# FFN begun on four row tiles, spectral middle lagged by one pair, pass two opened with gate halves: one change in three parts to a fused gradient kernel

## Chip, cores, metric

One core of one Trainium2 chip. The metric is the device time of one execution in microseconds (us), the median of several.

## The reference, cut to what matters

```python
x = A_x                                              # 2048 x 576, bf16
g = sigmoid((x * gate_w).sum(-1, keepdims=True))
a = irfft2(rfft2(x) * (w_r + 1j * w_i))              # spectral branch
b = (gelu(x @ w_gate) * (x @ w_up)) @ w_down         # FFN, 576 -> 4608 -> 576
out = g * a + (1 - g) * b
# the kernel returns out and the gradients of x, w_r, w_i, w_gate, w_up, w_down, gate_w
```

## The kernel before

Pass one walks 18 groups of 256 FFN columns; a group has 8 steps of two row tiles, 144 steps in all. A row tile is 128 rows. A step is 30 matmuls (`H_mm`), a chain of ScalarE and VectorE work (`H_ew1`, `H_ew2`) and three stores. Weight gradients of the last group (`pend`) and the spectral branch are threaded between the steps: `want` says how many of 203 spectral "slots" (small pieces of work; a "gap" is an empty one) must have been emitted by each half step, and `side` is a queue of VectorE items, of which some are emitted after each step. Pass two computes the down projection (b) and the gradient of x from stored activations, read back by DMA transposes (`pin`). Every engine runs its instructions in the order of emission.

The start, in which everything of x and of the output gradient is loaded and transposed first:

```python
for t0 in range(0, T, 4):
    nc.scalar.dma_start(xn[:, t0:t0 + 4, :], x_v[:, t0:t0 + 4, :])      # ScalarE issues x
...
wts = {0: load_w(0)}
for t in range(T):
    load_dOT(t)                       # two DMA transposes each, on the sync queue (LD)
...
for t0 in range(0, T, 4):
    LD.dma_start(dB[:, t0:t0 + 4, :], do_v[:, t0:t0 + 4, :])
...
build_D(nc, tb, unit, res)            # VectorE arguments, then ScalarE sines
x_chunk(0); build_R(nc, tb, unit, 0)
x_chunk(4); build_R(nc, tb, unit, 3)
x_chunk(8); build_R(nc, tb, unit, 6)
x_chunk(12)                           # then the gate of all 16 row tiles
```

The spectral middle. `s2` makes X and G of a pair of rows; after its last one the 12 product items of the pair go into `side`; `s1` transforms a product, and if it has not been emitted yet, it empties `side` up to it ("forced"):

```python
        side.extend(products(p))      # halve G, m1, m2, comb m, halve m + ready, n1, n2, comb n + ready, o1, o2, comb o, out
...
def s1(p, key, ii, dst):
    def f():
        while (p, key + "_ready") not in st:
            side.pop(0)()
        ...                           # four matmuls on st[p, key], ScalarE copy, store
for p in range(T // 2):
    out += [s2(p, "x", 0), s2(p, "x", 1), s2(p, "g", 0), s2(p, "g", 1)]
    out += [s1(p - 1, "n1", 0, scr_p2), s1(p - 1, "n1", 1, scr_p2)]      # three gaps for p = 0
    out += [s1(p, "m1", 0, scr_p1), s1(p, "m1", 1, scr_p1)]
...
for _ in range(3):                    # after each FFN step
    if side: side.pop(0)()
```

Pass two: seven pieces of the down projection (72 matmuls each) run first. Of the six loads of the transposed w_up (`wuT`) one goes ahead of the first piece and one behind each of the first five.

## Time and profile before

| | before |
|---|---|
| median time, us | 1625.99 (1625.65 to 1626.97, 4 runs) |
| span of the profiled run, us (a fifth run; its time was 1629.32) | 1627.5 |
| PE busy | 1523.0 us, 94% |
| granted TensorE clock, mean | 0.98 |
| start of FFN step 0 / 8 / 143 (square activation) | 38.0 / 124.6 / 1139.6 |
| end of the weight gradients | 1169.05 |

PE is nearly always busy, so the idle stretches, and the stretches at half clock that follow them, are what can be gained or lost. The square activation is the first ScalarE instruction of a step; its start times mark the steps and cut the kernel into stages that can be compared between versions. "Half clock" is taken from the clock record in the trace, which knows two values here, 1.0 and 0.5.

### The profile page before, as it was taken

What the parts mean: (1) busy time and instruction counts of PE and PEld (TensorE: products, weight loads), DVE (VectorE), ACT (ScalarE), POOL (GpSimd) and SP (SyncE); (2) the same over time, 40 slices, a digit from 0 to 9 for tenths busy, and PEclk for the clock granted to TensorE, in tenths of its full rate; (3) what the DMA queues carried; (4) which work ended last, traced back from release to release, by engine and by line L of the source; (5) the groups of instructions that cost most, each with busy time, mean ns of one, the idle gap of its engine ahead of it and who ended that gap; (6) DMA issues with size and microseconds to landing.
All of it is one profiled execution on the core that took longest, in us unless ns stands there. A gap on an engine that the chain in (4) does not pass through costs nothing.

```text
span 1627.5 us, 32888 instructions
## 1 busy us (share of the span) xinstructions
PE 1523.0 (94%) x13310; PEld 1276.6 (78%) x13310; DVE 893.2 (55%) x2287; ACT 628.1 (39%) x1096; POOL 26.3 (2%) x58
## 2 busy tenths in 40 slices
PE   4479999999899899899999999999898999999998
PEld 3357888888788788788888888888775777777776
DVE  3566767668789789777666667678123111111010
ACT  5355555545555555545545555545100000000000
POOL 1000000000000000000000000000000000000000
PEclk9789999999999999999999999999998999999999
DMA  6524234244434434334335345264799988887773
GB/s 131 136 65 112 80 103 111 80 121 130 128 116 143 124 118 140 103 109 123 109 94 135 103 116 130 87 156 127 212 208 211 171 172 159 165 165 162 149 150 70
DMA packets 512569, 212.66 MB, mean 131 GB/s; under 512 B 317984, under 2 KB 506272, under 8 KB 512416
## 3 DMA queue, kind: packets, MB, share of 16 engines
q1 hardware_dynamic: 510208, 203.48, 52.4%
q0 software_dynamic: 1632, 4.72, 0.8%
q10 hardware_dynamic: 576, 2.36, 0.6%
q8 instruction: 104, 1.70, 0.5%
q14 instruction: 49, 0.40, 0.1%
HBM read 40.89 MB, written 93.82 MB: 83 GB/s over the span
## 4 chain that ended last, share of the span: by engine, by line
PE 62%; issue 24%; DVE 5%; SPq 4%; ACT 3%; DMA 1%; POOL 1%; POOLq 0%; DVEq 0%; ACTq 0%
PE hps L286 25%; PE wps L365 15%; PE wps L349 7%; PE pf L610 3%; PE pf L405 3%; PE acc L780 2%; PE wps L376 2%; SPq L206 1%; SPq L207 1%; PE pf L596 1%; PE pf L594 1%; DMA pin<-scr 1%; SPq L720 1%; POOL out_dram L833 0%; ACT q L297 0%
## 5 line engine op out<-in xcount | busy, mean ns | idle before, releaser
L286 PEld LDWEIGHTS <-xT 128*128 128x128 bf16 x2880 | 286.3, 99 | 40.3
L822 PEld LDWEIGHTS <-pin 128*128 128x128 bf16 x2304 | 226.0, 98 | 61.6 <-DMA pin<-scr 3.8
L365 PEld LDWEIGHTS <-xn 128*128 128x128 bf16 x2304 | 223.9, 98 | 30.3 <-issue 3.6
L286 PE MATMUL hps<-wg_g,xT 128*128 128x256 bf16 x1440 | 187.0, 279 | 0.0
L286 PE MATMUL hps<-wu_g,xT 128*128 128x256 bf16 x1440 | 183.6, 275 | 0.0
L286 PE MATMUL hps<-wdT_g,dOT 128*128 128x256 bf16 x1440 | 181.1, 273 | 0.0
L299 DVE TENSOR_SCALAR s<-q 128x512 bf16<-128x512 bf16 x144 | 42.1, 292 | 229.0 <-ACT q L297 228.9
L780 PE MATMUL acc<-wd_all,pin 128*128 128x288 bf16 x1152 | 148.5, 293 | 13.1 <-DMA pin<-scr 13.1
L286 PEld LDWEIGHTS <-dOT 128*128 128x128 bf16 x1440 | 141.1, 98 | 16.6
L822 PE MATMUL acc<-wgT,pin 128*128 128x288 bf16 x1152 | 150.7, 288 | 3.5 <-DMA pin<-scr 3.5
L349 PE MATMUL wps<-dB,A 128*128 128x288 bf16 x1152 | 152.5, 287 | 0.0
L780 PEld LDWEIGHTS <-pin 128*128 128x128 bf16 x1152 | 114.5, 100 | 45.6 <-DMA pin<-scr 14.6
L822 PE MATMUL acc<-wuT,pin 128*128 128x288 bf16 x1152 | 149.1, 287 | 0.0
L830 DVE SCALAR_TENSOR_TENSOR f32t<-gwf,dlog,f32t 128x576 f32<-128x576 f32 x16 | 13.1, 818 | 238.3 <-ACT f32t L828 238.3
L349 PEld LDWEIGHTS <-A 128*128 128x128 bf16 x1152 | 112.7, 98 | 27.6
L365 PE MATMUL wps<-dHu,xn 128*128 128x256 bf16 x1152 | 131.7, 273 | 0.0
L365 PE MATMUL wps<-dHg,xn 128*128 128x256 bf16 x1152 | 131.5, 273 | 0.0
L297 ACT ACTIVATE q<-hps 128x512 bf16<-128x512 f32 x144 | 85.9, 597 | 111.3 <-PE hps L286 111.3
L828 ACT COPY f32t<-acc 128x576 f32<-128x576 f32 x16 | 10.2, 638 | 279.1 <-PE acc L822 279.1
L304 ACT ACTIVATE om<-s 128x512 bf16<-128x512 bf16 x144 | 91.0, 632 | 57.8 <-DVE s L300 57.8
L307 DVE TENSOR_TENSOR da<-hps,omg 128x512 bf16<-128x512 f32 x144 | 99.3, 690 | 2.8 <-PE hps L286 2.7
L305 ACT ACTIVATE s<-s 128x512 bf16<-128x512 bf16 x144 | 90.7, 630 | 4.6
(163 smaller groups left out, 1755.7 us busy)
## 6 DMA issues: line engine op xcount, KB each, us to landing
scr<-A SPq DMA_DIRECT2D x144, 128.0 KB, 1.8
scr<-dHg SPq DMA_DIRECT2D x144, 128.0 KB, 1.9
scr<-dHu SPq DMA_DIRECT2D x144, 128.0 KB, 1.9
out_dram<-dw SPq DMA_DIRECT2D x72, 128.0 KB, 1.9
out_dram<-dwd SPq DMA_DIRECT2D x36, 144.0 KB, 2.4
wd_all<-in_B_w_down_dram SPq DMA_DIRECT2D x3, 1728.0 KB, 13.5
scr_p<-Vt SPq DMA_DIRECT2D x32, 144.5 KB, 2.4
Vp<-scr_p SPq DMA_DIRECT2D x16, 289.0 KB, 3.0
```

The costliest lines, as they stand in the source:

```text
L286: nc.tensor.matmul(pt[:, tt, :], lhsT=xt[:, ci, tp * TPB + tt, :], rhs=w[:, ci, :], start=(ci == 0), stop=(ci == 4))
L297: nc.scalar.activation(q[:], hg[:], ACT.Square)
L299: V.tensor_scalar(s[:], q[:], A_GELU, 1.0, op0=ALU.mult, op1=ALU.add)
L304: nc.scalar.activation(om[:], s[:], ACT.Sigmoid, scale=-2.0 * C_GELU)
L305: nc.scalar.activation(s[:], s[:], ACT.Sigmoid, scale=2.0 * C_GELU)
L307: V.tensor_tensor(da[:], da_ps[:], omg32[:, t0:t0 + TPB].unsqueeze(2).to_broadcast([P, TPB, FG]), op=ALU.mult)
L349: nc.tensor.matmul(wps[:, :288], lhsT=tl(0, t)[:, fch * P:(fch + 1) * P], rhs=dB[:, t, h * 288:(h + 1) * 288], start=(t == 0), stop=(t == ...
L365: nc.tensor.matmul(wps[:, cc, :], lhsT=xn[:, t, (c0 + cc) * P:(c0 + cc + 1) * P], rhs=tl(k, t), start=(t == 0), stop=(t == T - 1))
L405: nc.tensor.matmul(yps[:, c, :DF], lhsT=src[:, ci, t, :], rhs=tb.Dt[ci][:, c, :], start=(ci == 0), stop=(ci == 4))
L610: nc.tensor.matmul(yps[:, h, :288], lhsT=Z[:, lc, c, :], rhs=tb.At[lc][:, c, h * 288:(h + 1) * 288], start=(n == 0), stop=(n == 5))
L780: nc.tensor.matmul(bps[:, h, :288], lhsT=At[:, r, :], rhs=wd_all[:, fc, h * 288:(h + 1) * 288], start=(fc == 0), stop=(fc == NFC - 1))
L822: nc.tensor.matmul(xps[:, h, :288], lhsT=src[:, r, :], rhs=wT[:, h * 288:(h + 1) * 288], start=(n < 2), stop=(n >= 4 * NFC - 2))
```

## The change

Its intent: begin the FFN when four row tiles of x are there and bring in the rest between the first steps; give each product of the spectral middle a pair's distance to its use; cover the loads of pass two with matmuls whose weights are already on the chip. The core of the diff, with cuts as `...` and long lines condensed:

```diff
-    build_D(nc, tb, unit, res)
-    x_chunk(0)
-    build_R(nc, tb, unit, 0)
-    ... (x_chunk 4, 8, 12, build_R 3, 6, gate of all tiles)
+    x_chunk(0, (0, 1, 2))
+    build_D(nc, tb, unit, res)
+    build_R(nc, tb, unit, 0)
+    run_late(tb)                        # sines are now emitted late, after the arguments
+    gate(0)
...
+    def early_x(k):                     # after steps 0, 1, 2: x chunk, gate, dOT; k == 3: dB loads
+    def early_tables():                 # after step 3
+        for t0 in range(3, T, 3):
+            build_R(nc, tb, unit, t0)
+        build_B(nc, tb, unit, res)
+        run_late(tb)
+        wts[1] = load_w(1)
...
     def want(step, half):
-        n = max(0.0, min(EARLY, 1.5 * (2 * step + half - 1)))     # EARLY = 24
-        h = 2 * (step - NT) + half
-        if h > 0:
-            n += (n_slots - EARLY) * h / (2.0 * (LAST - NT))
+        h = 2 * step + half
+        if h <= 2 * NT:
+            n = max(0, h - 3)
+        else:
+            n = 2 * NT - 3 + (n_slots - 2 * NT + 3) * (h - 2 * NT) / (2.0 * (LAST - NT))
...
-            out += [s1(p - 1, "n1", ...)] * 2 ; [s1(p, "m1", ...)] * 2
+            if p > 0:
+                out += [s1(p - 1, "m1", 0, scr_p1), s1(p - 1, "m1", 1, scr_p1)]
+                out += [s1(p - 1, "n1", 0, scr_p2), s1(p - 1, "n1", 1, scr_p2)]
...
-            for _ in range(3):
+            for _ in range(2):
                 if side:
...
-        LEAD = 7                        # pass two: b0 to b6, a wuT load ahead of b0 and behind b0 to b4
+    jobs = [("g", 0), ("g", 1), ("b", 0), ("b", 1), ("b", 2), ("u", 0), ("u", 1)]
+    ensure()                            # six pins, ahead of wd_all
+        for k in range(NB):
+            for r0 in (0, 6):
+                load_wuT(k, r0)         # all six, ahead of the first job
```

Beside these: the tile At of the inverse transform is stored in memory between its uses and one shared buffer fewer is kept (19), the absolute value in `build_D` moves from ScalarE to VectorE, dB is scaled in steps 6 to 9, x is loaded by the sync queue and not by ScalarE, a first small sine is run at once, some copies of the x chunks change engine, and the weight gradients of the first group run in another order.

More of the change, by code (lines that the diff above doesn't have):

```diff
@@ L35 @@
 FCH = FG // P
-NUNIT = 20
+NUNIT = 19
 IMM = bass.MemoryType
@@ L81, in iotas, with run_late @@
     nc.vector.memset(tb.npi[:], -math.pi * EPS_SCALE)
-    return tb
+    tb.warm = res.tile([P, 1], F32, name="warm")
+    nc.scalar.activation(tb.warm[:], tb.halfpi[:], ACT.Sin)
+    tb.late = []
+    return tb
+def run_late(tb):
+    while tb.late:
+        tb.late.pop(0)()
 def build_D(nc, tb, unit, res):
@@ L102, in build_D, with sines @@
         o = unit([n, 2, DF], name="Dt")
-        nc.scalar.activation(y[:], X[:], ACT.Abs)
-        nc.scalar.activation(o[:, :, 0, :], y[:], ACT.Sin, bias=tb.halfpi[:], scale=-step)
-        nc.scalar.activation(o[:, :, 1, :], X[:], ACT.Sin, scale=-step * EPS_SCALE)
+        V.scalar_tensor_tensor(y[:], X[:], -1.0, X[:], op0=ALU.mult, op1=ALU.max)
+        def sines(o=o, X=X, y=y):
+            nc.scalar.activation(o[:, :, 0, :], y[:], ACT.Sin, bias=tb.halfpi[:], scale=-step)
+            nc.scalar.activation(o[:, :, 1, :], X[:], ACT.Sin, scale=-step * EPS_SCALE)
+        tb.late.append(sines)
         tb.Dt += [o[:, c] for c in range(n)]
@@ L121, in build_R, with sines @@
     o = unit([n, 3, P], name="Rt")
-    nc.scalar.activation(o[:, :, 0, :], C[:], ACT.Sin, bias=tb.pi[:], scale=-step)
-    nc.scalar.activation(o[:, :, 1, :], X[:], ACT.Sin, bias=tb.npi[:], scale=step)
-    nc.scalar.activation(o[:, :, 2, :], X[:], ACT.Sin, bias=tb.pi[:], scale=-step)
+    def sines():
+        nc.scalar.activation(o[:, :, 0, :], C[:], ACT.Sin, bias=tb.pi[:], scale=-step)
+        nc.scalar.activation(o[:, :, 1, :], X[:], ACT.Sin, bias=tb.npi[:], scale=step)
+        nc.scalar.activation(o[:, :, 2, :], X[:], ACT.Sin, bias=tb.pi[:], scale=-step)
+    tb.late.append(sines)
     tb.Rt += [o[:, t] for t in range(n)]
@@ L146, in build_B, with sines @@
     step = 2.0 * math.pi / 16 * EPS_SCALE
-    nc.scalar.activation(o[:, 0, :], XC[:, 0, :], ACT.Sin, bias=tb.npi[:], scale=step)
-    nc.scalar.activation(o[:, 1, :], XC[:, 1, :], ACT.Sin, bias=tb.pi[:], scale=-step)
-    nc.scalar.activation(o[:, 2, :], XC[:, 0, :], ACT.Sin, bias=tb.pi[:], scale=-step)
     tb.B = res.tile([P, 3, P], BF16, name="Btab")
-    V.tensor_tensor(tb.B[:], o[:], mask[:].unsqueeze(1).to_broadcast([P, 3, P]), op=ALU.mult)
+    def sines():
+        nc.scalar.activation(o[:, 0, :], XC[:, 0, :], ACT.Sin, bias=tb.npi[:], scale=step)
+        nc.scalar.activation(o[:, 1, :], XC[:, 1, :], ACT.Sin, bias=tb.pi[:], scale=-step)
+        nc.scalar.activation(o[:, 2, :], XC[:, 0, :], ACT.Sin, bias=tb.pi[:], scale=-step)
+        V.tensor_tensor(tb.B[:], o[:], mask[:].unsqueeze(1).to_broadcast([P, 3, P]), op=ALU.mult)
+    tb.late.append(sines)
 @with_exitstack
@@ L181 @@
     scr_x = dram.tile([T, P, 2, DF], BF16, name="scr_x")
+    scr_at = dram.tile([3, P, 2, D], BF16, name="scr_at")
     scr_g = dram.tile([T, P, 2, DF], BF16, name="scr_g")
@@ L186 @@
     xn = res.tile([P, T, D], BF16, name="xn")
-    for t0 in range(0, T, 4):
-        nc.scalar.dma_start(xn[:, t0:t0 + 4, :], x_v[:, t0:t0 + 4, :])
     gwT = res.tile([P, 5], BF16, name="gwT")
@@ L212 @@
     tb = iotas(nc, res, unit)
-    wts = {0: load_w(0)}
     with nc.allow_non_contiguous_dma(reason="tiny gate_w column load"):
@@ L216, with load_x, load_do, load_dOT @@
         nc.gpsimd.dma_start(gwT[:, 4:5], gate_w[DCH[4][0]:D].rearrange("(p o) -> p o", o=1))
-    for t in range(T):
-        load_dOT(t)
-        if t % 2 == 1:
-            nc.gpsimd.memset(dOT[0:D4NEW, 4, t - 1:t + 1, :], 0.0)
-    for t0 in range(0, T, 4):
-        LD.dma_start(dB[:, t0:t0 + 4, :], do_v[:, t0:t0 + 4, :])
-    wts[1] = load_w(1)
+    def load_x(t0):
+        LD.dma_start(xn[:, t0:t0 + 4, :], x_v[:, t0:t0 + 4, :])
+    def load_do(t0):
+        LD.dma_start(dB[:, t0:t0 + 4, :], do_v[:, t0:t0 + 4, :])
+    def load_dOT(t0):
+        for t in (t0, t0 + 1):
+            LD.dma_start_transpose(dOT[:, 0:4, t, :], do_v[:, t, 0:512])
+            LD.dma_start_transpose(dOT[:, 4:5, t, :], do_v[:, t, DCH[4][0]:D])
+        nc.gpsimd.memset(dOT[0:D4NEW, 4, t0:t0 + 2, :], 0.0)
+    load_x(0)
+    wts = {0: load_w(0)}
+    load_dOT(0)
+    for k in range(1, 4):
+        load_x(4 * k)
+        load_dOT(2 * k)
     gwb = res.tile([P, D], BF16, name="gwb")
-    LD.dma_start(gwb[:], gate_w.partition_broadcast(P))
     ew = wstack.enter_context(tc.tile_pool(name="ew", bufs=2))
@@ L240, with x_chunk @@
     omg32 = res.tile([P, T], F32, name="omg32")
-    lps = pw.tile([P, 512], F32, tag="wps", name="lps")
     tb.Rt = []
-    def x_chunk(t0):
+    def x_chunk(t0, act):
         for k, c0 in enumerate((0, 2, 4)):
@@ L253, in x_chunk, with gate @@
             o, i = xT[p0:, c0:c0 + nc_, t0:t0 + 4, :], tp_[p0:, 0:nc_]
-            if k == 1:
+            if k in act:
+                nc.scalar.copy(o, i)
+            else:
                 V.tensor_copy(o, i)
-            else:
-                nc.scalar.copy(o, i)
+    def gate(t0):
+        lps = pw.tile([P, 512], F32, tag="wps", name="lps")
         for t in range(t0, t0 + 4):
             for ci in range(5):
-                nc.tensor.matmul(lps[:, t:t + 1], lhsT=xT[:, ci, t, :], rhs=gwT[:, ci:ci + 1],
+                nc.tensor.matmul(lps[:, t - t0:t - t0 + 1], lhsT=xT[:, ci, t, :], rhs=gwT[:, ci:ci + 1],
                                  start=(ci == 0), stop=(ci == 4))
+        sl = slice(t0, t0 + 4)
+        nc.scalar.activation(g_bf[:, sl], lps[:, 0:4], ACT.Sigmoid)
+        V.tensor_copy(g32[:, sl], g_bf[:, sl])
+        V.tensor_scalar(omg_bf[:, sl], g32[:, sl], -1.0, 1.0, op0=ALU.mult, op1=ALU.add)
+        V.tensor_copy(omg32[:, sl], omg_bf[:, sl])
+    x_chunk(0, (0, 1, 2))
     build_D(nc, tb, unit, res)
-    x_chunk(0)
     build_R(nc, tb, unit, 0)
-    x_chunk(4)
-    build_R(nc, tb, unit, 3)
-    x_chunk(8)
-    build_R(nc, tb, unit, 6)
-    x_chunk(12)
-    nc.scalar.activation(g_bf[:], lps[:, 0:T], ACT.Sigmoid)
-    V.tensor_copy(g32[:], g_bf[:])
-    V.tensor_scalar(omg_bf[:], g32[:], -1.0, 1.0, op0=ALU.mult, op1=ALU.add)
-    V.tensor_copy(omg32[:], omg_bf[:])
+    run_late(tb)
+    gate(0)
     kept = {}
@@ L381, in u_tail @@
             LD.dma_start(out_5[512:576, fsl], dw[64:128, :])
-        us = [u_dwd(fch, h) for fch in range(FCH) for h in range(2)]
-        us += [u_dw(1, o4v, c0) for c0 in range(0, 4, TPB)]
+        us = [u_dw(1, o4v, c0) for c0 in range(0, 4, TPB)]
+        ud = [u_dwd(fch, h) for fch in range(FCH) for h in range(2)]
+        us = us + ud if g == 0 else ud + us
         us += [u_tail]
@@ L441, in f, with load_At @@
                 nc.gpsimd.memset(o[0:L2NEW, :, :], 0.0)
-            tb.At.append(o)
-        return f
-    def late_tables():
-        for t0 in range(9, T, 3):
-            build_R(nc, tb, unit, t0)
-        build_B(nc, tb, unit, res)
+            LD.dma_start(scr_at[lc], o[:])
+        return f
+    def load_At():
+        for lc in range(3):
+            o = unit([2, D], name="At")
+            LD.dma_start(o[:], scr_at[lc])
+            tb.At.append(o)
+    load_At.noslot = True
     def zipped(u1, u2):
@@ L565, in mid_units @@
         out = [first] + [gap] * 3
-        for p in range(T // 2):
-            out += [s2(p, "x", 0), s2(p, "x", 1), s2(p, "g", 0), s2(p, "g", 1)]
-            if p > 0:
-                out += [s1(p - 1, "n1", 0, scr_p2), s1(p - 1, "n1", 1, scr_p2)]
+        NPAIR = T // 2
+        for p in range(NPAIR + 1):
+            if p < NPAIR:
+                out += [s2(p, "x", 0), s2(p, "x", 1), s2(p, "g", 0), s2(p, "g", 1)]
             else:
                 out += [gap] * 3
-            out += [s1(p, "m1", 0, scr_p1), s1(p, "m1", 1, scr_p1)]
-        p = T // 2 - 1
-        out += [s1(p, "n1", 0, scr_p2), s1(p, "n1", 1, scr_p2)]
+            if p > 0:
+                out += [s1(p - 1, "m1", 0, scr_p1), s1(p - 1, "m1", 1, scr_p1)]
+                out += [s1(p - 1, "n1", 0, scr_p2), s1(p - 1, "n1", 1, scr_p2)]
         return out
@@ L632 @@
     mid = mid_units()
-    fft = fx[:4] + at + fx[4:] + fg + mid[:-2] + pa + mid[-2:] + [gap] * 2 + ia[:-4] + pb + ia[-4:] + ib
+    fft = fx[:4] + at + fx[4:] + fg + mid[:-2] + [load_At] + pa + mid[-2:] + [gap] * 2 + ia[:-4] + pb + ia[-4:] + ib
     fft_pos = [0]
@@ L646 @@
     LAST = NG * NT - 16
-    EARLY = 3 * NT
     done = [0]
     def want(step, half):
-        n = max(0.0, min(EARLY, 1.5 * (2 * step + half - 1)))
-        h = 2 * (step - NT) + half
-        if h > 0:
-            n += (n_slots - EARLY) * h / (2.0 * (LAST - NT))
+        h = 2 * step + half
+        if h <= 2 * NT:
+            n = max(0, h - 3)
+        else:
+            n = 2 * NT - 3 + (n_slots - 2 * NT + 3) * (h - 2 * NT) / (2.0 * (LAST - NT))
         return int(min(n, n_slots) + 1e-9)
@@ L670, in load_wgT, with f @@
             wgT_all.extend([u[:, 0], u[:, 1]])
+    def early_x(k):
+        def f():
+            x_chunk(4 * k, (0, 1))
+            gate(4 * k)
+            if k < 3:
+                load_dOT(4 + 4 * k)
+                load_dOT(6 + 4 * k)
+            if k == 3:
+                for t0 in range(0, T, 4):
+                    load_do(t0)
+        return f
+    def early_tables():
[4 more added lines that the diff above has]
+        wts[1] = load_w(1)
+        LD.dma_start(gwb[:], gate_w.partition_broadcast(P))
+    early = {0: early_x(1), 1: early_x(2), 2: early_x(3), 3: early_tables}
     wgT_from = 108
@@ L682 @@
             H_ew2(g, tp, tiles)
-            if g == 0:
-                for t in (2 * tp, 2 * tp + 1):
+            if step in early:
+                early[step]()
+            if 6 <= step < 6 + T // 4:
+                for t in range(4 * (step - 6), 4 * (step - 6) + 4):
                     V.tensor_scalar(dB[:, t, :], dB[:, t, :], omg32[:, t:t + 1], None, op0=ALU.mult)
-                if tp == 2:
-                    late_tables()
             if done[0] == n_slots or (step >= wgT_from and step % 4 == 0 and len(wgT_all) < 20):
@@ L708, with pin, ensure @@
     wd_all = p2r.tile([P, NFC, D], BF16, name="wd_all")
-    wuT = [p2r.tile([P, FCB, D], BF16, name="wuT0")]
+    p2in = ctx.enter_context(tc.tile_pool(name="p2in", bufs=6, side="right", **kw))
     wd_v = B_w_down.rearrange("(r p) d -> p r d", p=P)
+    def pin(k, t, f0):
+        tl = p2in.tile([P, FCB, P], BF16, tag="pin", name="pin")
+        LD.dma_start_transpose(tl[:], scr[k][t // TPB][t % TPB][:, f0 * P:(f0 + FCB) * P])
+        return tl
+    jobs = [("g", 0), ("g", 1), ("b", 0), ("b", 1), ("b", 2), ("u", 0), ("u", 1)]
+    for t in range(2, T):
+        jobs += [("g", t), ("u", t)] + ([("b", t + 1)] if t + 1 < T else [])
+    seq = [("bgu".index(kind), t, f0) for kind, t in jobs for f0 in range(0, NFC, FCB)]
+    loaded = {}
+    cur = [0]
+    used = [0]
+    def ensure():
+        while cur[0] < min(used[0] + 6, len(seq)):
+            loaded[seq[cur[0]]] = pin(*seq[cur[0]])
+            cur[0] += 1
+    ensure()
     for f0 in range(0, NFC, FCB):
@@ L727 @@
          tc.tile_pool(name="p2b", bufs=8, **kw) as p2b, \
-         tc.tile_pool(name="p2in", bufs=6, **kw) as p2in, \
          tc.tile_pool(name="p2s", bufs=4, **kw) as p2s, \
@@ L732 @@
          tc.tile_pool(name="pgw", bufs=1, space=PSUM, **kw) as pgw:
-        wuT += [p2res.tile([P, FCB, D], BF16, name=f"wuT{k}") for k in range(1, NB)]
+        wuT = [p2res.tile([P, FCB, D], BF16, name=f"wuT{k}") for k in range(NB)]
         dlog = p2res.tile([P, T], F32, name="dlog")
@@ L737 @@
         V.tensor_copy(gwf[:], gwb[:])
-        wT_loads = [(k, r0) for k in range(NB) for r0 in (0, 6)]
-        def pin(k, t, f0):
-            tl = p2in.tile([P, FCB, P], BF16, tag="pin", name="pin")
-            LD.dma_start_transpose(tl[:], scr[k][t // TPB][t % TPB][:, f0 * P:(f0 + FCB) * P])
-            return tl
+        for k in range(NB):
+            for r0 in (0, 6):
+                load_wuT(k, r0)
         def f32t():
@@ L749, in b16t @@
             return p2b.tile([P, D], BF16, tag="b16t", name="b16t")
-        LEAD = 7
-        jobs = [("b", t) for t in range(LEAD)]
-        for t in range(T):
-            jobs.append(("x", t))
-            if t + LEAD < T:
-                jobs.append(("b", t + LEAD))
-        seq = []
-        for kind, t in jobs:
-            seq += [(k, t, f0) for f0 in range(0, NFC, FCB) for k in ((0,) if kind == "b" else (1, 2))]
-        loaded = {}
-        cur = [0]
-        used = [0]
-        def ensure():
-            while cur[0] < min(used[0] + 6, len(seq)):
-                loaded[seq[cur[0]]] = pin(*seq[cur[0]])
-                cur[0] += 1
         def b_job(t):
@@ L809, in gate_grad, with x_half, x_end @@
             ST.dma_start(out_7.rearrange("(o d) -> o d", o=1), dgw[:].rearrange("o h d -> o (h d)"))
-        def x_job(t):
-            xps = pacc.tile([P, 2, 512], F32, tag="acc", name="acc")
+        accs = {}
+        def x_half(t, k):
+            if k == 1:
+                accs[t] = pacc.tile([P, 2, 512], F32, tag="acc", name="acc")
+            xps = accs[t]
+            for f0 in range(0, NFC, FCB):
+                src = loaded.pop((k, t, f0))
+                for r in range(FCB):
+                    wT = wgT_all[f0 + r] if k == 1 else wuT[f0 // FCB][:, r]
+                    for h in range(2):
+                        nc.tensor.matmul(xps[:, h, :288], lhsT=src[:, r, :], rhs=wT[:, h * 288:(h + 1) * 288],
+                                         start=(k == 1 and f0 + r == 0), stop=(k == 2 and f0 + r == NFC - 1))
+                used[0] += 1
+                ensure()
+        def x_end(t):
+            xps = accs.pop(t)
             dxa_t = b16t()
             LD.dma_start(dxa_t[:], dxa_v[:, t, :])
-            n = 0
-            for f0 in range(0, NFC, FCB):
-                for k in (1, 2):
-                    src = loaded.pop((k, t, f0))
-                    for r in range(FCB):
-                        wT = wgT_all[f0 + r] if k == 1 else wuT[f0 // FCB][:, r]
-                        for h in range(2):
-                            nc.tensor.matmul(xps[:, h, :288], lhsT=src[:, r, :], rhs=wT[:, h * 288:(h + 1) * 288],
-                                             start=(n < 2), stop=(n >= 4 * NFC - 2))
-                            n += 1
-                    used[0] += 1
-                    ensure()
             xo = f32t()
@@ L833, in x_job @@
             ST.dma_start(o1v[:, t, :], o1[:])
-        ensure()
-        load_wuT(*wT_loads.pop(0))
         for kind, t in jobs:
@@ L839 @@
                 b_job(t)
-                if wT_loads:
-                    load_wuT(*wT_loads.pop(0))
-            else:
-                x_job(t)
-                if t == T - 3:
+            elif kind == "g":
+                x_half(t, 1)
+            else:
+                if t == T - 1:
                     gate_grad()
+                x_half(t, 2)
+                x_end(t)
 _INS = ['A_x', 'A_w_r', 'A_w_i', 'B_x', 'B_w_gate', 'B_w_up', 'B_w_down', 'gate_w', 'grad_out']
```

## The prediction

> **What bounds the kernel now.** I read the page first, then the busy times in stretches of 20 us and in stretches cut where the work changes, then who waited for whom, then the order of instructions in the first 100 us and around the change of passes.
>
> ```profile
> span 1627.5 us, 32888 instructions
> PE 1523.0 (94%) x13310; PEld 1276.6 (78%) x13310; DVE 893.2 (55%) x2287; ACT 628.1 (39%) x1096; POOL 26.3 (2%) x58
> ```
>
> PE is busy for 94%, so only its idle time (about 104 us) and its slow-clock time can be won; the change removes no large PE work. The stretches say where both lie (columns: stretch, length, busy us of PE, PEld, DVE, ACT, POOL, granted clock, DMA share, GB/s). I cut them at the first matmul work of the FFN (about 38), at the ninth FFN step (124.6, the ninth start of the square activation L297), around the spectral middle (368.4 to 700), at the end of the weight gradients (1169.05) and where pass two becomes steady.
>
> ```profile
> 0.00:38.00 38.00, 14.57 (x172) 12.48 (x173) 13.84 (x42) 20.35 (x31) 6.45 (x21) 1.00 0.63 136
> 38.00:124.60 86.60, 54.20 (x409) 41.69 (x408) 52.29 (x149) 41.88 (x74) 1.99 (x4) 0.82 0.36 100
> 124.60:368.40 243.80, 239.90 (x2175) 206.26 (x2173) 164.78 (x428) 130.32 (x231) 0.00 (x0) 1.00 0.37 101
> 368.40:700.00 331.60, 310.29 (x2765) 265.00 (x2763) 275.70 (x701) 177.91 (x318) 0.00 (x0) 0.98 0.44 126
> 700.00:1169.05 469.05, 469.05 (x4311) 407.61 (x4309) 308.12 (x805) 237.22 (x413) 0.00 (x0) 1.00 0.45 123
> 1169.05:1272.60 103.55, 86.94 (x649) 65.94 (x650) 23.42 (x58) 4.47 (x7) 3.79 (x7) 0.92 1.10 203
> ```
>
> PE idles 23 + 32 us before 124.6, 4 us up to 368, 21 us in the spectral middle, nothing up to 1169 and 17 us where pass two opens. The three parts of the change aim at exactly these three holes. The waits of PE name them; the first two lines are from the first 125 us, the next two from 125 to 1169, the last two from 1140 to 1300.
>
> ```profile
> PE lps L260 <- ACT xT L257: 18.1, 6, 15.6
> PE pf L419 <- ACT Y L409: 17.1, 6, 13.4
> ...
> PE pf L553 <- DVE m L509: 14.5, 5, 5.0
> PE pf L486 <- ACT Xx L494: 4.8, 3, 2.5
> ...
> PE acc L780 <- DMA pin<-scr: 13.1, 5, 5.6
> PE acc L822 <- DMA pin<-scr: 3.5, 1, 3.5
> ```
>
> Behind the first is ScalarE, which issues the four loads of x, is free only at 14.18 us and then makes all sine tables before the copies of xT. Behind the second is VectorE: its scaling of dB waits 11.7 us for a load that stands in the sync queue behind 32 DMA transposes of about 1.25 us each. The order of instructions shows both, and the sync queue at the opening of pass two:
>
> ```profile
> 0.75 13.40 ACTq L188 DMA_DIRECT2D xn<-in_A_x_dram  x4
> 14.18 1.28 ACT L103 ACT_TABLE_LOAD   x1 [14.18 <-DMA wdT_g<-in_B_w_down_dram]
> 56.38 0.65 DVE L685 TENSOR_SCALAR dB<-dB,omg 128x576 bf16<-128x576 bf16 x2 [11.71 <-DMA dB<-in_grad_out_dram]
> ...
> 1170.24 11.12 SPq L742 DMA_TRANSPOSE pin<-scr  x6
> 1181.40 4.63 SPq L720 DMA_TRANSPOSE wuT<-in_B_w_up_dram  x1
> ```
>
> **What the Trainium skill says.** "TensorE: Matmul & The Clock Gate", Part 1, has PE fall to half clock after an idle window of about 3.4 us and recover after as long a busy one. The trace agrees: after the 5.65 us wait at 1169 the clock record shows 6.8 us at 0.5, and after the wait of 4.02 us at 1224.5 a job of 72 matmuls took 11.68 us instead of 8.99. The specification table at the head of that page calls ScalarE and VectorE strict first-in first-out, 64-deep reordering being TensorE's alone; so one late operand blocks everything emitted after it, as the dB wait shows. "DMA: Bandwidth & Descriptors", Queues, rings and completion order, has each DMA engine consume a ring in order; so what the sync queue issues later queues behind earlier bytes. Trace: a pin landed 4.2 us after issue in the median, a wuT piece 7.0 us, a dwd store 7.1 us behind wd_all against 2.4 us elsewhere. "ScalarE: Activation LUTs", What ACT_TABLE_LOAD costs, gives about 1283 ns a table load; the trace shows 1.28 us.
>
> **Part one, the start.** Removed: three of the four x chunks, the whole gate, ten of the sixteen row tiles' dOT transposes and the four dB loads from ahead of the first step. ScalarE no longer issues loads. New start, by durations of the trace: x tile block 0 lands at about 5 us as before; its 20 transposes take 2.3, the three ScalarE copies 1.0 + 1.0 + 0.6, so xT is there at 9. VectorE builds D in 7.6 us as before plus about 2.3 us for the absolute value moved to it (estimate from 0.52 us for 289 columns) and R in 1.75, so it ends at about 13; ScalarE's sines trail it (3.9 + 1.8 us) to 15; table load 1.28 and sigmoid: the first square of the FFN at 16.7 us against 38.0 before.
>
> Then the steps. A step's chain from the square to dHu is 6.6 us (38.0 to 44.6 before). In steps 0 to 2 an x chunk hangs on it serially: its third copy stands behind dHu on VectorE (0.45), then come 20 gate matmuls (0.8), and the next step's matmuls stand behind those on PE (1.2 to 2.3 by clock). So 9.4, 9.1 and, with the first spectral slots, 11 us: step 3 starts at 46. Step 3 ends with the R and B tables: VectorE 7.4 + 1.8 us, ScalarE trailing to 10.3 us after the step's end, so 17 us, and step 4 starts at 63. Steps 4 to 7 have two spectral slots each in place of three (7.4 to 8.4 us a step before); VectorE's 5.3 us and a slot chain make 6.5 to 7, the first 8.2 for the sigmoid table: 28.5. Step 8 starts at about 92 instead of 124.6: −32.6 us. The new pacing has issued 13 slots by then instead of 22.5; the 9.5 others come later, where PE is full: 1.25 us and 0.5 us of matmuls alternately, 0.9 in the mean, +8.5 us.
>
> **Part two, the middle.** m1 is now consumed a pair later, when its products have long been emitted, so the 14.5 us that PE waited for `DVE m L509` go. Also most of the slow clock that those waits cause: the record shows 13.7 us at 0.5 between 399 and 695, worth about 6 us. Of 25 us idle between 124.6 and 1169 I leave 9: the 0.8 us waits for the single spectral PSUM buffer, and some waits for n1, because two products a step instead of three leave about 10 pops for the 12 items of a pair and the rest are forced just before use. Moving At through memory adds 3 stores and 3 loads that nothing waits for. 25.2 − 9 + 6 − 1 = −21 us.
>
> **Part three, pass two.** Here I expect nothing, perhaps a loss. Bytes are unchanged: wd_all and wuT 5.3 MB each, three pins of 393 KB per 72 matmuls. Before, six of seven pieces of work each carried one wuT piece (4.05 to 5.5 us on the sync queue) and three pins (5.5 to 7), 11.5 us against 8.99 of PE; the idle was 16.6 us and the slow clock cost some 7 more. Now the six pins are issued at 1146.8 (11 us), ahead of wd_all, so PE goes straight on at 1169 and works 17.7 us on the two gate halves. But wd_all is 11 us later (it took some 18 us to land), the last stores of dw wait behind it until about 1180, and all six wuT pieces stand in the queue before the first pin of the down projection: 6 × 4.4 = 26.4 us, then 5 us to landing. That is about 1211, where PE ran dry at 1187: one wait of some 22 to 25 us, and 2.7 us of slow clock. Jobs b0 to b2 share one accumulator, as two are held by half-done rows: +1.8 us. Together +4 us.
>
> **Sum.** −32.6 + 8.5 − 21 + 4 = −41 us: a span of 1586, and with the time as far below the span as now, about 1583.
>
> **Rivals.** (a) The new opening of pass two works as meant: the gate halves cover all loads, no wait over 5 us. For it: warm PE at 1169, and PE gets 18 us more cover. Against: the place of the wuT loads in the sync queue. It would give −20 us more: about 1562. (b) VectorE becomes the bound in the middle: it is busy for 276 of 332 us there, and the pacing after step 8 is 6% denser in slots. The waits then only change name, from m to n or to the square's PSUM; the gain of part two shrinks to 5 us: about 1599. (c) The serial x chunks and a cold PE make steps 0 to 3 as slow as before and step 8 starts at 105: about 1595. (d) The start is better than I chain it, step 8 at 80: about 1570.
>
> **Range and chances.** (b) and (c) together stay near 1610, (a) and (d) near 1552; each alone is about one chance in five. So 1558 to 1604. The 2% line is 1593.2, some 11 us above my figure, with a spread of about 16: faster 0.74, same 0.25, slower 0.01.
>
> **What would show it.** Right: first square near 17 us, the ninth near 92; no wait of 4 us for the products in the middle and a clock of 1.00 there; no PE wait at the end of the weight gradients, then one long wait for a pin of the down projection after the gate halves, the sync queue full of wuT just before it. Wrong: the ninth square after 100, waits for n in place of m, or no such wait in pass two.

## The result, and the profile after

Median 1655.54 us (1652.75 to 1656.93, 4 runs) against 1625.99. The ratio is 1.0179, interval 1.0161 to 1.0196: slower, though by less than 2%. A ratio here is the mean time of one kernel's runs over that of the other's of the same rounds, so not quite the ratio of the medians quoted. The prediction (1583, range 1558 to 1604) was wrong in sign.

The page of the changed kernel, then its busy times in stretches (length, PE, PEld, DVE, ACT, POOL busy, clock, DMA share, GB/s), cut at: first square, ninth square (101.4), spectral middle and what follows it in three pieces, end of the weight gradients (1194.35), opening of pass two.

```profile
span 1653.4 us, 32899 instructions
PE 1529.4 (92%) x13310; PEld 1278.4 (77%) x13310; DVE 895.5 (54%) x2298; ACT 627.9 (38%) x1097; POOL 26.6 (2%) x58
```

```profile
16.20:101.40 85.20, 48.41 (x445) 39.23 (x443) 55.80 (x165) 45.16 (x80) 3.39 (x8) 0.78 0.52 132
101.40:345.70 244.30, 243.49 (x2209) 209.60 (x2208) 166.72 (x440) 133.51 (x235) 0.00 (x0) 1.00 0.35 100
345.70:684.00 338.30, 299.27 (x2572) 249.80 (x2570) 246.27 (x625) 162.95 (x292) 0.00 (x0) 0.95 0.39 114
684.00:816.30 132.30, 122.36 (x1073) 103.40 (x1072) 92.65 (x236) 64.45 (x113) 0.00 (x0) 0.96 0.39 113
816.30:1194.35 378.05, 377.32 (x3462) 327.69 (x3460) 246.02 (x644) 190.33 (x332) 0.00 (x0) 1.00 0.49 127
1194.35:1260.00 65.65, 43.94 (x334) 33.50 (x333) 7.52 (x18) 1.86 (x3) 1.09 (x2) 0.84 1.00 220
```

The same 13310 matmuls; PE idles a further 20 us and is busy 6 us longer. By stage, each number the difference of two marks (before / after):

| stage | before | after | difference | predicted |
|---|---|---|---|---|
| to step 8 | 124.6 | 101.4 | −23.2 | −32.6 |
| step 8 to step 143 | 1015.0 | 1063.5 | +48.5 | −12.5 (+8.5 − 21) |
| step 143 to the end | 487.9 | 488.5 | +0.6 | +4 |
| sum | 1627.5 | 1653.4 | +25.9 | −41 |

The medians differ by 29.6 us, not 25.9, mainly because the profiled run of the kernel before was a slow one by 3.3 us. Part of that seems to lie in pass two: in experiment 4, which has the same pass two, it took 454.0 us from the end of the weight gradients, against 458.45 in the profile used here. Against that run the +0.6 would be 5.1.

The start gained, pass two changed little, and the loss is in the middle. The stage from step 8 to step 143, before, changed, and in experiment 1 below:

```profile
124.60:1139.60 1015.00, 989.79 (x8972) 853.66 (x8970) 741.92 (x1917) 539.89 (x950) 0.00 (x0) 0.99 0.42 116
101.40:1164.90 1063.50, 1013.00 (x9032) 865.03 (x9031) 744.99 (x1929) 546.26 (x960) 0.00 (x0) 0.98 0.40 112
102.10:1110.70 1008.60, 991.25 (x9033) 857.09 (x9031) 743.94 (x1929) 544.55 (x960) 0.00 (x0) 1.00 0.43 118
```

Of the +48.5 us, 25.3 are idle time of PE (25.2 before, 50.5 after). The clock record shows half clock there for 44.4 us against 13.7; half of that difference, 15.4 us, explains most of the other 23.2, and the 60 matmuls that the new pacing moved out of the start the rest. The waits of PE from 320 to 800 us in the changed kernel (a line names what waited, who released it, the us in total, the number of waits and the longest):

```profile
PE pf L582 <- DVE m L538: 26.0, 7, 5.1
PE pf L582 <- DVE n L552: 16.4, 8, 3.8
```

The waits for m, which the lag was to remove, rose from 14.5 to 26.0 us, and waits for n joined them. The longest of them, in order of time (start, duration, engine, line, operation, and in brackets the idle time before it and its releaser):

```profile
540.93 0.76 DVE L546 TENSOR_TENSOR m<-Xx,Wt 128x1156 bf16<-128x1156 bf16 x1
...
547.53 0.76 DVE L546 TENSOR_TENSOR m<-Xx,Wt 128x1156 bf16<-128x1156 bf16 x1
548.32 0.47 DVE L552 TENSOR_TENSOR m<-m,m 128x578 bf16<-128x578 bf16 x1
...
549.19 0.18 DVE L538 TENSOR_SCALAR m<-m 128x8 bf16<-128x8 bf16 x1
549.43 0.42 PE L582 MATMUL pf<-m,Rt 128*128 128x289 bf16 x1 [5.08 <-DVE m L538]
```

Between the two products of m stands a whole FFN step of VectorE work (542.33 to 547.61). The second product and the combination are the two items popped after that step, and the tiny halving (0.18 us) was emitted only when the matmul asked for it.

At the start, the tables after step 3 are where the plan slipped:

```profile
56.37 2.04 SPq L237 DMA_DIRECT2D dB<-in_grad_out_dram  x4
58.51 0.48 SPq L452 DMA_DIRECT2D scr_x<-Vt  x1
...
66.78 0.28 DVE L158 TENSOR_SCALAR maskB<-k_i,cf 128x128 f32<-128x128 int32 x1 [6.28 <-DMA scr_x<-Vt]
67.10 0.61 ACT L135 ACTIVATE Rt<-CR,pi 128x384 bf16<-128x384 int32 x1 [16.25 <-DVE maskB L158]
```

VectorE stands still 6.28 us for a buffer that a small store must free. The store was issued behind transposes and the dB loads, and landed 8.2 us after its issue (2.2 in the median of this line); ScalarE then begins its sines only after VectorE's last table instruction, 16.25 us after it was ready, although the first arguments were done at 53. The opening of pass two runs as predicted:

```profile
1171.98 11.92 SPq L763 DMA_TRANSPOSE pin<-scr  x6
1183.94 6.43 SPq L781 DMA_DIRECT2D wd_all<-in_B_w_down_dram  x3
...
1204.55 23.02 SPq L789 DMA_TRANSPOSE wuT<-in_B_w_up_dram  x6
1227.66 10.96 SPq L763 DMA_TRANSPOSE pin<-scr  x6
```

```profile
1232.38 11.56 PE L827 MATMUL acc<-wd_all,pin 128*128 128x288 bf16 x72 [19.21 <-DMA pin<-scr]
```

One wait of 19.2 us behind the six wuT loads takes the place of six waits of 16.6 us. The clock record has 20.5 us at half clock in place of 17.1, but most of them now pass while PE stands idle: PE was busy at half clock for 5.3 us in place of 13.7. So PE's idle time in pass two rose by 5.1 us and its busy time fell by 4.5.

### The profile page after: what moved, and what is told of

Read it like the earlier page. It is cut to its first block, busy times and chain, and to the rows that moved or that the text cites. A ratio compares the mean times of both kernels' runs of the same rounds, so it can differ in the third digit from the quotient of the medians.

```text
span 1653.4 us, 32899 instructions
## 1 busy us (share of the span) xinstructions
PE 1529.4 (92%) x13310; PEld 1278.4 (77%) x13310; DVE 895.5 (54%) x2298; ACT 627.9 (38%) x1097; POOL 26.6 (2%) x58
## 4 chain that ended last, share of the span: by engine, by line
PE 61%; issue 23%; DVE 8%; ACT 3%; SPq 2%; DMA 2%; POOL 1%; POOLq 0%; DVEq 0%; ACTq 0%
PE hps L312 25%; PE wps L391 15%; PE wps L375 7%; PE pf L639 3%; PE pf L432 2%; PE wps L402 2%; PE acc L827 2%; PE acc L869 2%; SPq L789 1%; PE pf L623 1%; PE pf L625 1%; DVE s L326 1%; SPq L763 1%; DVE q L328 1%; ACT q L323 1%
## 5 line engine op out<-in xcount | busy, mean ns | idle before, releaser
L312 PEld LDWEIGHTS <-xT 128*128 128x128 bf16 x2880 | 290.0, 101 | 43.8
L312 PE MATMUL hps<-wg_g,xT 128*128 128x256 bf16 x1440 | 191.6, 283 | 0.0
L827 PE MATMUL acc<-wd_all,pin 128*128 128x288 bf16 x1152 | 146.3, 289 | 20.7 <-DMA pin<-scr 19.2
L375 PE MATMUL wps<-dB,A 128*128 128x288 bf16 x1152 | 156.8, 291 | 0.0
L827 PEld LDWEIGHTS <-pin 128*128 128x128 bf16 x1152 | 113.8, 99 | 51.1 <-DMA pin<-scr 19.5
L869 PE MATMUL acc<-wgT,pin 128*128 128x288 bf16 x1152 | 143.7, 286 | 1.0 <-DVE dw L359 1.0
L869 PE MATMUL acc<-wuT,pin 128*128 128x288 bf16 x1152 | 143.6, 286 | 0.0
L879 ACT COPY f32t<-acc 128x576 f32<-128x576 f32 x16 | 10.2, 639 | 257.7 <-PE acc L869 257.7
## 6 DMA issues: line engine op xcount, KB each, us to landing
scr_p<-Vt SPq DMA_DIRECT2D x32, 144.5 KB, 2.1
```

What stands on the lines that cost most here:

```text
L312: nc.tensor.matmul(pt[:, tt, :], lhsT=xt[:, ci, tp * TPB + tt, :], rhs=w[:, ci, :], start=(ci == 0), stop=(ci == 4))
L375: nc.tensor.matmul(wps[:, :288], lhsT=tl(0, t)[:, fch * P:(fch + 1) * P], rhs=dB[:, t, h * 288:(h + 1) * 288], start=(t == 0), stop=(t == ...
L827: nc.tensor.matmul(bps[:, h, :288], lhsT=At[:, r, :], rhs=wd_all[:, fc, h * 288:(h + 1) * 288], start=(fc == 0), stop=(fc == NFC - 1))
L869: nc.tensor.matmul(xps[:, h, :288], lhsT=src[:, r, :], rhs=wT[:, h * 288:(h + 1) * 288], start=(k == 1 and f0 + r == 0), stop=(k == 2 and ...
```

## The experiments

Each was timed in three rounds against the kernel before on the same chip. Its median over the four sets of rounds was 1625.4 to 1625.5, so medians below compare directly. Edits are condensed, with `...` for what is left out.

**1. Three pops in place of two.**

```diff
-            for _ in range(2):
+            for _ in range(3):
```

> The changed kernel with three product items popped per FFN step in place of two, nothing else. Theory P (pace): a pair of the middle takes 8 slots, about 5 steps, so two pops a step emit about 10 of its 12 items; the rest is always forced just before PE needs it, and the lag is worth nothing. Then PE's waits for m (26.0 us) and n (16.4 us) fall below 8 us together, the slow clock in the middle goes, and the time falls by 35 to 45 us, to 1610 to 1620. Rival V (VectorE is simply full in the middle, or the lag holds too many buffers): the waits change name or stay, time within 10 us of 1655.

Measured 1602.21 us (1601.58 to 1603.12), 53 us below the changed kernel and at 0.9856 of the kernel before. The longest waits of PE from step 8 to the end of the weight gradients:

```profile
PE pf L515 <- ACT Xx L523: 4.8, 3, 2.1
PE pf L582 <- ACT Vt L587: 3.6, 3, 1.8
PE pf L582 <- ACT Xg L525: 2.5, 2, 1.7
```

No wait is put down to m or n any more, and the clock record shows no half clock from step 8 to step 143. From step 8 to step 143 it took 1008.6 us against 1063.5; PE was busy 991.3 against 1013.0 us for the same work, the difference being about half of the 44.4 us at half clock. Theory P holds, beyond its range; V falls.

To see why, I replayed the queue from the source, counting items popped by force (arithmetic on the program, not a run):

```
order, pops, pacing          forced items of m, pairs 0..7     of n
changed: lag, 2, new         0 1 1 1 1 1 1 3                   0 1 1 1 1 1 1 0
lag, 3, new                  none                              none
no lag, 2, new               1 2 2 2 2 2 2 3                   none
before: no lag, 3, old       none                              none
```

A pair takes 8 slots, about 5 steps, in which two pops a step emit some 10 of 12 items, so the queue never runs empty and the last item of m or n is forced for most pairs. Being forced is not the whole of it, though: nothing was forced for the first pair, which yet waited 4.3 us for m (at 417.15), nor for any pair of the kernel before, which waited 14.5 us in all. There the item left the queue at the end of the step before its use, behind that step's VectorE work.

**2. The old order, two pops kept.**

```diff
-            if p > 0: [s1(p-1,"m1")]*2 + [s1(p-1,"n1")]*2
+            [s1(p-1,"n1")]*2 + [s1(p,"m1")]*2
```

> The changed kernel with the old order of the middle (m1 of a pair consumed in its own pair), two pops kept. Theory P: the same queue is as late as before and m1 is forced for all eight pairs with five items at once: waits for m of 25 to 40 us, time 1645 to 1675. Rival L (the lag itself costs, by buffers held longer or by the order of slots): undoing it brings the middle back to the kernel before, time near 1615.

Measured 1617.42 us (1615.41 to 1619.05). My expectation fell, and the figure is rival L's: with too few pops the old order is 38 us better than the lag. Its waits:

```profile
PE pf L582 <- DVE m L538: 19.5, 8, 4.2
...
PE pf L582 <- DVE n L552: 1.2, 1, 1.2
```

In the old order six slots lie between the m and the n of a pair, so one pop by force serves both; with the lag they are two slots apart and both are forced. The replay shows just that (no n forced); that it is the order of slots and not the buffers held longer is argued from it and from experiment 3, where the lag costs nothing. Half clock fell from 44.4 to 10.2 us.

**3. Old order and three pops** (edits 1 and 2 together).

> The changed kernel with the old order of the middle and the old three pops a step: the middle of the kernel before inside the new start and the new pass two. Theory P: the lag is worth something once the products keep pace, so without it the waits for m of the kernel before return (14.5 us, some 10 us of slow clock with them) and the time is 1612 to 1622, 10 to 20 us above the run with lag and three pops (1602). Rival: the pace alone did it, and the time is 1600 to 1606.

Measured 1601.99 us (1600.51 to 1603.30), waits for m 4.3 us, none over 2.3: no different from the lag with three pops. So in the changed kernel's pacing the lag is worth nothing once the pops keep up. Theory P in this point fell, and a new question arose: why are the waits for m 4.3 us here and 14.5 in the kernel before, with the same order and pops?

**4. The kernel before with two pops** (edit 1 in reverse, in the kernel before).

> The kernel before with two pops a step in place of three, nothing else. Theory F (in the old order a pair has one forced point, at m; only the lag puts m and n close together and forces both): waits for m rise from 14.5 to about 20 us, n stays under 3 us, time 1628 to 1636. Rival N (two pops cost the same in any order): time 1655 to 1670.

Measured 1639.57 us (1639.33 to 1643.04), ratio 1.0091. Waits for m 24.3 us, n 1.8, half clock from step 8 to step 143 23.9 us against 13.7. The direction is F's, the size (14 us) above its range: two pops cost the kernel before 14 us and the lagged kernel 53.

**5. Old order, three pops and the old pacing of the slots** (in the changed kernel).

```diff
-        h = 2 * step + half
-        n = h - 3 up to step 8, then evenly
+        n = min(24, 1.5 * (2 * step + half - 1)), then evenly from step 8
```

> The changed kernel with the old order of the middle, three pops and also the old pacing of the spectral slots (24 slots early, then the rest evenly): all of the kernel before but its start, its pass two and the room for At. Theory A (the waits for m depend on where a pair's slots fall in the eight steps of a group, and the new pacing happens to move them): the waits for m return from 4.3 us to 10 to 16 us, with 7 to 14 us of slow clock, time 1606 to 1616. Rival U (the three unit buffers that At no longer holds made m early): waits for m stay under 6 us, time 1599 to 1604.

Measured 1620.16 us (1616.86 to 1621.32). The waits for m are back:

```profile
PE pf L582 <- DVE m L538: 14.4, 5, 5.0
```

with 17.1 us of half clock. So the pacing, which I had counted only as slots moved to later, is what removed most of the waits, and U falls. That it did so by shifting the slots of a pair against the FFN steps is supported by the replay and the trace, not by a run of its own: in the replay the old pacing asks for m in the first half of the step after the one that made it ready for four of the eight pairs, the new pacing for none (always in the second half of a step). The three long waits here (4.1, 4.0 and 5.0 us, at 428, 550 and 673) are three of those four, each in the third step of a group; the fourth of these pairs did not wait. The time is above A's range by 4 us, and most of the 18.2 us against experiment 3 is not these waits: step 8 starts at 114.6 in place of 102.2, with 24 slots in 8 steps again, and the stage from step 8 to step 143 is 4.9 us longer.

**6. The same with the lag** (old pacing, three pops, lag).

> The run with old order, old pacing and three pops (1620 us), plus the lag of one pair. Theory G (the lag is a sound cure where the waits for m exist; with the new pacing and three pops there was nothing left to cure): waits for m fall from 14.4 to under 4 us, n stays under 3 us, slow clock in the middle from 17 to under 8 us, time 1604 to 1612. Rival W (the lag does not cure them, VectorE has no room in those steps whatever the distance): m and n together stay above 9 us, time 1615 to 1623.

Measured 1609.75 us (1609.36 to 1612.76). No wait for m or n, 6.8 us of half clock: theory G holds. The lag is thus a sound cure for a wait that exists: 10 us here, though a wait of 7.0 us for a load of `Vp` took part of the gain. The changed kernel and the five runs in its frame (new start, new pass two):

| order | pops | pacing | us | waits for m / n |
|---|---|---|---|---|
| lag | 2 | new | 1655.5 | 26.0 / 16.4 |
| lag | 3 | new | 1602.2 | 0 / 0 |
| old | 2 | new | 1617.4 | 19.5 / 1.2 |
| old | 3 | new | 1602.0 | 4.3 / 0 |
| old | 3 | old | 1620.2 | 14.4 / 0 |
| lag | 3 | old | 1609.8 | 0 / 0 |

**7. Sines emitted after each table.**

```diff
         for t0 in range(3, T, 3):
             build_R(nc, tb, unit, t0)
+            run_late(tb)
         build_B(nc, tb, unit, res)
         run_late(tb)
```

> The changed kernel with the sines of the late tables emitted after each table in step 3 instead of after all of them. Theory S (the sines are emitted late, so they are released late and their inputs hold their buffers, whence VectorE's 6.3 us wait before maskB): the first late sine moves from 67.1 to about 53 us, maskB no longer waits, the fifth square moves from 74.9 to 62 to 65 us, time 8 to 12 us lower, 1644 to 1648. Rival D (the wait of maskB for a store is only the sync queue being late, whatever the sines do): R sines move, maskB still runs at 66.8, the fifth square at about 69, time 4 to 6 us lower.

Measured 1651.05 us (1647.75 to 1653.21), 4.5 below the changed kernel, whose lowest run was 1652.75: Rival D's size, but little above the spread of the runs. In the trace step 8 came 2.4 us sooner (99.0) and the fifth square at 72.3. The first late sine ran at 56.8 us, but VectorE's wait only moved to another table instruction:

```profile
DVE XR L128 <- DMA scr_x<-Vt: 8.4, 1, 8.4
```

**8. The dB loads after step 4 in place of step 2.**

```diff
-            if k == 3:
-                for t0 in range(0, T, 4): load_do(t0)        # after step 2
+    early = {..., 4: early_do}                                # the same four loads
```

> The changed kernel with the four loads of dB moved from the end of step 2 to the end of step 4, nothing else. Theory D (VectorE waits before maskB because the buffer is freed by a store of the spectral forward pass that stands in the sync queue and in the rings behind 2.4 MB of dB): maskB runs at 60.5 in place of 66.8, the fifth square at 67 to 69 in place of 74.9, time 5 to 8 us lower, 1648 to 1651. Rival: the store is late for the sixteen dOT transposes before it alone; maskB moves by less than 2 us and the time stays within 3 us of 1655.

Measured 1649.04 us (1648.74 to 1649.65), 6.5 lower: theory D. VectorE no longer waits for the store. It was issued 1.9 us sooner (56.59), still behind the transposes, and landed 2.2 us after its issue in place of 8.2; so the four dB loads just before it, more than the queue of transposes, had made it late. The fifth square came at 71.0, later than the expected 67 to 69, and maskB at 62.8. ScalarE still began at 63.15, right after maskB, 9.85 us after it was ready. So there were two causes, one behind the other. Why sines that are emitted late wait for the last table instruction and not for their own arguments is not shown by any run; that emitting them early cures it is.

**9. The wuT loads spread over pass two's opening.**

```diff
-        load all six wuT pieces ahead of the first job
+        one piece after g0, g1, b0; two after b1; one after b2
```

> The changed kernel with the six wuT pieces of pass two issued one or two after each of the first five pieces of work, not all ahead of the first pin of the down projection. Theory Q (order in the sync queue): the one wait of 19.2 us for a pin and the slow clock behind it go; some waits of at most 8 us in sum stay for pins and wuT pieces; time 14 to 22 us lower, 1633 to 1641. Rival B (bytes: the DMA engines are full there anyway): the same 19 us reappear as several waits, time within 5 us of 1655.

Measured 1653.21 us (1651.40 to 1653.46), 2.3 lower: Rival B's time. The wait for pins went, but the wuT pieces came too late for the first up half:

```profile
PE acc L868 <- DMA wuT<-in_B_w_up_dram: 14.1, 3, 9.4
```

The sync queue is full there: a piece of work needs three pins (5.4 us), a wuT piece (4.3) and 1.0 of small loads against 8.98 us of matmuls.

**10. The same, with six pieces of the down projection before the first up half** (`b0` to `b5`, one wuT piece behind each of the first six pieces of work).

> The changed kernel with only pass two changed: six pieces of the down projection before the first up half, one wuT piece behind each of the first six pieces of work. Theory Q' (the wait is there because the six wuT pieces stand in a row ahead of pins; with more work on PE between them they hide): no wait over 4 us where pass two opens, no more than 8 us of slow clock there, time 10 to 15 us below the changed kernel, 1640 to 1645. Rival B (what was gained with all the edits together is not of pass two): time within 5 us of 1655.

Measured 1644.16 us (1642.19 to 1645.76), 11.4 lower, half clock there 6.8 us. Waits for pins are 9.0 us in four, none over 3.1. Theory Q' holds. From the end of the weight gradients to 1260 us the DMA engines moved as much per us as before (214 against 220 GB/s) and were as full (share 1.09 against 1.00). So the row of wuT loads made the long wait, and enough matmul work between the loads removes most of it. Whether the bytes or the issue time of the queue set what is left is not separated by these runs.

**11. All together:** three pops, sines after each table, dB after step 4, the opening of experiment 10.

> The changed kernel with everything that the runs point to: three pops, sines after each table, the dB loads after step 4, and in pass two six pieces of the down projection ahead of the first up half with one wuT piece behind each of the first six pieces of work. If the causes add: 53 us from the pops, 8 to 12 from the tables, 10 to 15 from pass two (waits for pins and wuT under 8 us in sum): 1572 to 1585, the fifth square at 62 to 65 us. If pass two is bound by bytes or by the sync queue whatever the order, its waits stay above 12 us and the time is 1588 to 1596.

Measured 1577.71 us (1576.24 to 1578.78), ratio 0.9705, interval 0.9691 to 0.9719: better than both kernels. The 77.8 us below the changed kernel are close to the sum of the single runs (53.3 + 4.5 + 6.5 + 11.4 = 75.7). By stages of the profiles they are 52.5 from step 8 to step 143 (1011.0 against 1063.5), 10.5 before step 8 (90.9 in place of 101.4) and 13.8 in pass two (445.3 us from the end of the weight gradients against 459.05). The fifth square ran at 64.7.

## Why the prediction was wrong, point by point

- **First square near 17 us:** right, 16.2 (38.0 before). Steps 1 to 3 as chained: 25.4, 36.8, 45.5 against 26.1, 35.2 and 46.
- **Tables after step 3, 17 us:** wrong, 29.4 (45.5 to 74.9). The step took ScalarE to trail VectorE; instead the sines waited for the whole of VectorE's tables, and VectorE for a store. Experiments 7, 8 and 11 show both: without them the stage took 17.0 us (47.7 to 64.7), as predicted.
- **Steps 4 to 7, 28.5 us:** 26.5. Step 8 at 92: 101.4, and 90.9 with the tables mended.
- **Deferred slots, +8.5 us:** about right; 23.2 us of added busy time less 15.4 of clock leaves 7.8. But the same new pacing did something that the prediction did not see: by itself it took the waits for m from 14.4 to 4.3 us (experiments 3 and 5), it seems by moving slots against steps.
- **Middle, −21 us:** the step that failed, and the reason that the stage from step 8 to step 143 lost 48.5 us in place of gaining 12.5. It said that m "is now consumed a pair later, when its products have long been emitted" and put the forced items of n within 9 us of left-over idle. The two numbers that refute it were in the prediction itself: about 10 pops for 12 items. A queue that gets 12 and gives 10 never catches up, so a later use is just as late, and the last item comes behind a whole step of VectorE work. Waits of 42.4 us and 44.4 us of half clock came of it; experiment 1 gives back 53 us by one number. The size was too hopeful as well: with three pops the stage gains 6.4 us (1008.6 against 1015.0) and 17.3 us of idle stay, not 9, and by experiment 3 even that is not the lag's doing.
- **Rival (b), VectorE as the bound:** it saw the symptom ("from m to n") but not the cause. VectorE was busy 744 to 745 us from step 8 to step 143 in both the changed kernel and experiment 1, in 1063.5 and 1008.6 us: it had room, the order of its queue was at fault.
- **Pass two, +4 us:** right in mechanism, and in size as far as the profiles tell: +0.6, or some 5 against the pass two of experiment 4. The fall in PE's slow busy time from "some 7" to 2.7 us of cost came as said (half of 13.7, half of 5.3). The wait was 19.2 us in place of 22 to 25, since six wuT pieces alone took 23.0 us and not 26.4; rival (a) fell. The shared accumulator cost two waits of 0.73 us, 1.5 against 1.8.
- Rivals (c) and (d), which only moved step 8, bracket the outcome (101.4 between 80 and 105); neither mattered beside the middle.
- **Its own signs:** two of the three that were to show it wrong came, the ninth square after 100 (101.4) and waits for n, these beside m and not in its place.
- **Slips that did no harm:** before the first copies of xT ScalarE makes the tables of `build_D`, not all sine tables (those of R begin at 23.54, after the first two copies). And "the time as far below the span as now" set the median beside the span of another, slower run; within one run the time is about 1.8 us above the span (1629.32 and 1627.5).

## What to carry to other kernels

When work for one engine is handed out from a queue at a fixed rate, compare the rate with the arrivals first: where it was below, moving the consumer later bought nothing here, and with two consumers close together both waited. A store that frees a buffer is as late as its place in the issuing queue and the bytes issued just before it make it; before moving loads forward, ask which small store they will stand in front of. And the loads here hid only where matmul work stood between them: an opening with resident weights helps once, then the row of loads behind it must fit as well.

## What the Trainium skill lacked or had wrong

- "TensorE: Matmul & The Clock Gate", Part 1, says the ramp penalty is below 1% of a typical kernel span. It says so of the warm-up, and treats repeated ramps further on, so this is a figure not to be taken too widely more than an error: in the changed kernel the 44.4 us at half clock in the middle alone, in ten stretches, cost 21.8 us of busy time for the same work (1013.0 against 991.3 us), 1.3% of the span. The two states and steps of 3.4 us agree with the page.
- "DMA: Bandwidth & Descriptors", Issuing engines are not separate DMA queues, calls the sequencer's time to issue usually small relative to the DMA. For DMA transposes it is not: in the median of the kernel before, each of the dOT pieces held the sync queue 1.23 or 1.26 us and landed 2.5 or 2.8 us after issue, and in the changed kernel six wuT pieces held it 23.0 us.
- No page gives a size for what a small store loses behind large loads in the same queue: the 144.5 KB store landed 8.2 us after its issue behind four loads of 576 KB, and 2.2 us with them moved away (experiment 8). VectorE waited 6.3 us for the buffer in the changed kernel, 8.4 in experiment 7.
